# A fused attention and SwiGLU kernel: probabilities as the stationary operand, chunks of 256 queries, and an order from a list scheduler in the builder

## The chip, the cores and the metric

The kernel runs on one core of one Trainium2 chip. The metric is device time in microseconds (us), lower is better. Three runs of the kernel before stood at the outset: median 364.23 us, from 361.57 to 364.9.

Short names: PE is the matmul engine, PEld its weight load, DVE the vector engine, ACT the scalar engine, POOL the GpSimd engine, SP the engine whose queue stores the output. "AV" is the product of the attention probabilities with V; "FFN" is the gated network after the attention.

## The reference

Four batches, eight heads, 768 positions, head width 64. Attention has a block mask of 32x32 blocks (neighbours, first and last block row and column, three sampled blocks for each row). The result goes through an RMS norm and a gated network without bias. In short form:

```python
scores = scale * np.matmul(q, k.transpose(0, 1, 3, 2))     # 4 x 8 x 768 x 768
scores = np.where(mask, scores, -1000000000.0)
attn = np.exp(scores - np.max(scores, axis=-1, keepdims=True))
attn = attn / (np.sum(attn, axis=-1, keepdims=True) + 1e-09)
attn_out = np.matmul(attn, v)
x = attn_out.transpose(0, 2, 1, 3).reshape(B * S, H * D)   # 3072 x 512
rms = np.sqrt(np.mean(x * x, axis=-1, keepdims=True) + 1e-06)
xn = x / rms * rms_g
g = xn @ w_gate                                            # 512 x 1536
out = (g * (1.0 / (1.0 + np.exp(-g))) * (xn @ w_val)) @ w_out
```

## The kernel before

It works in eight units of 384 queries. For each pair of heads it computes the transposed scores (keys on the partitions, queries in the columns), takes the exponential on ACT, multiplies by a 0/1 mask on DVE, and then uses the result as the moving operand of AV:

```python
    def qk_mm(n, jt):
        # ... cut ...
        for e in range(2):                       # two heads: two 64-row halves of the array
            nc.tensor.matmul(
                out=s_[:, e, 0:TG],              # TG = 384 queries
                lhsT=x[64 * e:64 * e + 64, 1, jt, pr, :],
                rhs=x[64 * e:64 * e + 64, 0, ic * NT:(ic + 1) * NT, pr, :],
                start=True, stop=True)

    def av(n, shared):
        # ... cut ...
        for jt in range(NC):
            for e in range(2):
                nc.tensor.matmul(
                    out=o_[64 * e:64 * e + 64, :],
                    lhsT=vb[:, 2 * pr + e, jt * D:(jt + 1) * D],     # V is stationary, 64 columns
                    rhs=pt_[:, jt, e, :], start=(jt == 0), stop=(jt == NC - 1),
                    skip_group_check=True)
        nc.scalar.copy(out=osb[u][:, pr, :], in_=o_)
        # ... cut ...
```

The result has the head dimension on the partitions and the queries in the columns, as the FFN wants it. But the sum of a query's probabilities is then a sum over partitions. It takes matmuls of its own, which stream all probabilities through the array a second time:

```python
    def zsum(n):
        # ... cut ...
        for j2 in range(NC // 2):
            for e in range(2):
                for par in range(2):
                    c = 2 * e + par
                    nc.tensor.matmul(
                        out=zwt[u][32 * c:32 * c + 32, :], lhsT=Ez[:, pr, :],
                        rhs=pt_[:, 2 * j2 + par, e, :],
                        start=(pr == 0 and j2 == 0), stop=False, skip_group_check=True)
```

Five more functions (norm_a to norm_e) turn these sums and the squares into one factor per query and head, transpose the factors with matmuls (zt, ft), spread them over the partitions with matmuls (fb), and multiply. The FFN then runs with 384 moving columns for gate and value (gp, vp) and 512 for the output (yp). The order of work on PE is fixed by hand: steps with a list of costs, with the FFN of the unit before filling the gaps.

```python
        at(s1 + 1, 1.25, av, n, n >= 8)
        at(s1 + 1, 0.7, zsum, n)
```

The softmax here doesn't subtract the row's maximum and nothing guards it: scores larger than these inputs give would overflow.

## Time and profile before

| | before |
|---|---|
| time, median of the runs | 364.23 us |
| span of the profiled execution | 362.5 us |
| PE busy | 333.8 us (92%) |
| first FFN matmul (gp) starts | 54.94 us |
| one unit of 384 queries, steady | 40.0 us |

The profile's page gives, in this order: the span, the busy time of each engine, the PE's busy tenths in 40 slices with the clock granted to PE in the same slices, and the shares by engine of the chain that ended last.

```profile
span 362.5 us, 6294 instructions
...
PE 333.8 (92%) x2454; PEld 159.1 (44%) x2454; DVE 246.9 (68%) x531; ACT 222.6 (61%) x354; POOL 84.5 (23%) x112
...
PE   2787789899799999999999999999999999999995
...
PEclk9998988999999999999999999999999999999999
...
PE 75%; ACT 11%; DVE 7%; issue 4%; DMA 1%; POOL 1%; POOLq 0%; ACTq 0%; DVEq 0%
```

One warning for every clock figure of these views: time for which the trace has no clock record is counted as full clock. In this trace the record begins at 23.8 us, and the first two digits of the clock row say nothing.

PE is busy nearly everywhere after the first quarter, and the chain that ended last is 75% PE. The first quarter is worse: 2, 7, 8, 7, 7, 8, 9 tenths. The table of windows confirms it for two stretches of 40 us. Its columns are the stretch, its length, the busy time of PE, PEld, DVE, ACT and POOL (instructions in brackets), the granted clock, the DMA share and the GB/s.

```profile
180.00:220.00 40.00, 39.34 (x297) 18.87 (x293) 28.79 (x62) 27.61 (x45) 8.56 (x9) 1.00 0.56 90
220.00:260.00 40.00, 39.34 (x297) 18.87 (x293) 28.79 (x62) 27.61 (x45) 5.00 (x5) 1.00 0.06 21
```

39.34 of 40 us on PE, at full clock, against less than 29 on every other engine: in this state only less PE work, or the small rest, can gain time. The timeline shows what PE works on. Its columns are the start, the duration (both us), the engine, the line, the operation and its shapes. Durations of single matmuls contain a modelled end, so a cost is read from one start to the next.

```profile
200.61 1.17 PE L281 MATMUL o__2597<-pt,vb 128*64 128x384 bf16 x12
...
201.71 0.67 PE L297 MATMUL zw<-pt,Ez 128*32 128x384 bf16 x12
...
202.31 0.34 PE L248 MATMUL s__2626<-qkT 64*128 64x384 bf16 x2
...
202.48 0.33 PE L248 MATMUL s__2630<-qkT 64*128 64x384 bf16 x2
...
202.74 0.39 PE L419 MATMUL yp<-wo,hp 128*128 128x512 bf16 x1
```

AV takes 201.71 - 200.61 = 1.10 us per pair of heads and unit, the sums zw 202.31 - 201.71 = 0.60 us. The second score tile takes 0.26 us to the next full-array matmul where the first took 0.17 to the second: the other 0.09 us is a turn from 64-row score work to full-array work. The first FFN work, in the same view:

```profile
54.06 0.32 PE L368 MATMUL fb_726<-fs,SelB 128*128 128x384 bf16 x1 [0.20 <-DVE xn L373]
54.94 1.46 PE L388 MATMUL gp<-xn,wg 128*128 128x384 bf16 x4
```

Until 54.94 us there is no FFN work to fill PE's gaps.

### The profile page before, as it was taken

How to read it: one execution, taken by the hardware profiler on the slowest of the kernel's cores; microseconds unless marked ns; L12 is line 12 of the kernel's file. 1: busy time of each engine (PE TensorE's matmuls, PEld its weight loads, DVE VectorE, ACT ScalarE, POOL GpSimd, SP SyncE). 2: the span in 40 equal slices, each digit the busy share in tenths (PEclk: the TensorE clock that was granted, in tenths of full speed). 3: DMA queues.
4: the chain of work that ended last, by engine and by line, in shares of the span. 5: the costliest groups of instructions: out<-in, count | busy, mean ns of one | idle time of the engine just before them, and what ended most of it. 6: DMA issues, size and time to landing. Idle time of an engine off the chain costs nothing.

```text
span 362.5 us, 6294 instructions
## 1 busy us (share of the span) xinstructions
PE 333.8 (92%) x2454; PEld 159.1 (44%) x2454; DVE 246.9 (68%) x531; ACT 222.6 (61%) x354; POOL 84.5 (23%) x112
## 2 busy tenths in 40 slices
PE   2787789899799999999999999999999999999995
PEld 1233334344344444455444444454444444555552
DVE  3577786778666786687667785687767776666540
ACT  2465876777676667667666766766676675323321
POOL 8930620135331201143440311021011111100000
PEclk9998988999999999999999999999999999999999
DMA  5999999349661491067770390000000000000012
GB/s 64 171 213 198 157 189 159 72 29 59 44 40 36 104 161 55 32 43 74 73 61 15 62 225 33 32 0 32 29 29 1 31 29 3 30 31 29 33 56 88
DMA packets 69026, 25.58 MB, mean 71 GB/s; under 512 B 57220, under 2 KB 64900, under 8 KB 68996
## 3 DMA queue, kind: packets, MB, share of 16 engines
q0 software_dynamic: 46352, 14.16, 36.9%
q1 hardware_dynamic: 22644, 11.02, 13.0%
q8 instruction: 19, 0.31, 0.4%
q14 instruction: 11, 0.09, 0.1%
HBM read 28.31 MB, written 6.29 MB: 95 GB/s over the span
## 4 chain that ended last, share of the span: by engine, by line
PE 75%; ACT 11%; DVE 7%; issue 4%; DMA 1%; POOL 1%; POOLq 0%; ACTq 0%; DVEq 0%
PE yp L419 16%; PE gp L388 15%; PE vp L405 12%; ACT pt L256 6%; PE zw L297 5%; PE oa L281 3%; ACT th L392 3%; DVE uu L394 2%; DVE pt L262 1%; PE zt L317 1%; DMA kb<-in_k_dram 1%; PE fb L368 1%; DVE xn L373 1%; PE vw L405 1%; PE gw L388 1%
## 5 line engine op out<-in xcount | busy, mean ns | idle before, releaser
L262 DVE TENSOR_TENSOR pt<-pt,Mk 128x768 bf16<-128x768 bf16 x192 | 101.1, 571 | 0.4
L394 DVE SCALAR_TENSOR_TENSOR uu<-th,gp 128x384 bf16<-128x384 bf16 x90 | 49.8, 554 | 61.7 <-ACT th L392 61.4
L388 PE MATMUL gp<-xn,wg 128*128 128x384 bf16 x360 | 74.0, 328 | 3.1 <-DVE uu L394 2.9
L419 PE MATMUL yp<-wo,hp 128*128 128x512 bf16 x288 | 76.1, 380 | 0.0
L392 ACT ACTIVATE th<-gp 128x384 bf16<-128x384 f32 x90 | 44.4, 493 | 49.8 <-PE gp L388 46.8
L405 PE MATMUL vp<-xn,wv 128*128 128x384 bf16 x360 | 73.4, 326 | 0.7 <-DVE hp L408 0.6
L408 DVE TENSOR_TENSOR hp<-uu,vp 128x384 bf16<-128x384 bf16 x90 | 49.6, 551 | 10.2 <-PE vp L405 4.7
L388 PEld LDWEIGHTS <-wg 128*128 128x128 bf16 x384 | 35.5, 98 | 39.4 <-issue 14.5
L405 PEld LDWEIGHTS <-wv 128*128 128x128 bf16 x384 | 35.4, 98 | 29.9 <-issue 9.7
L419 PEld LDWEIGHTS <-hp 128*128 128x128 bf16 x288 | 26.1, 98 | 29.1 <-issue 7.7
L248 PEld LDWEIGHTS <-qkT 64*128 64x128 bf16 x384 | 13.9, 94 | 47.1 <-issue 45.5
L281 PEld LDWEIGHTS <-vb 128*64 128x64 bf16 x384 | 24.5, 115 | 16.8 <-issue 11.1
L425 ACT ACTIVATE yo<-yp 128x512 f32<-128x512 f32 x24 | 14.3, 597 | 13.6 <-PE yp L419 12.1
L297 PE MATMUL zw<-pt,Ez 128*32 128x384 bf16 x384 | 22.6, 344 | 0.0
L373 DVE SCALAR_TENSOR_TENSOR xn<-osb,gcol,fb 128x384 bf16<-128x384 f32 x28 | 15.9, 609 | 8.2 <-PE fb L368 8.2
L79 POOL DMA_DIRECT2D qb<-in_q_dram x18 | 16.4, 909 | 7.7 <-DMA wg<-in_moe_w_gate_dram 7.5
L79 POOL DMA_DIRECT2D qb<-in_k_dram x18 | 16.2, 901 | 7.1 <-DMA wv<-in_moe_w_val_dram 6.5
L332 POOL TENSOR_TENSOR rs<-ms,nhalf 128x3 f32<-128x3 f32 x8 | 7.1, 891 | 39.9 <-DVE ms L329 39.9
L297 PEld LDWEIGHTS <-Ez 128*32 128x32 bf16 x384 | 7.5, 97 | 12.8 <-issue 11.2
L281 PE MATMUL oa<-pt,vb 128*64 128x384 bf16 x96 | 12.6, 413 | 0.2 <-DVE Mk L199 0.2
L287 POOL TENSOR_TENSOR o_3107<-osb 128x384 bf16<-128x384 f32 x4 | 4.1, 1032 | 29.2 <-ACT osb L286 29.2
L287 POOL TENSOR_TENSOR o_2595<-osb 128x384 bf16<-128x384 f32 x4 | 4.1, 1030 | 28.3 <-ACT osb L286 28.3
(556 smaller groups left out, 415.6 us busy)
## 6 DMA issues: line engine op xcount, KB each, us to landing
out_dram<-yo SPq DMA_DIRECT2D x24, 256.0 KB, 2.0
vb<-in_v_dram POOLq DMA_DIRECT2D x4, 768.0 KB, 9.0
qb<-in_q_dram POOLq DMA_DIRECT2D x18, 128.0 KB, 4.5
qb<-in_k_dram POOLq DMA_DIRECT2D x18, 128.0 KB, 4.6
wg<-in_moe_w_gate_dram POOLq DMA_DIRECT2D x1, 1536.0 KB, 14.1
wv<-in_moe_w_val_dram POOLq DMA_DIRECT2D x1, 1536.0 KB, 20.7
wo<-in_moe_w_out_dram POOLq DMA_DIRECT2D x1, 1536.0 KB, 18.5
qb<-in_q_dram POOLq DMA_DIRECT2D x2, 192.0 KB, 3.6
```

The source lines that it names most:

```text
L79: nc.gpsimd.dma_start(out=flat[:, c * DM:(c + 1) * DM].rearrange("p (h d) -> p h d", h=H), in_=src[b, :, :, c * D:(c + 1) * D])
L256: nc.scalar.activation(out=ptiles[n][:, jt, :, :], in_=s_[:, :, 0:TG], func=AF.Exp, scale=SCALE)
L262: nc.vector.tensor_tensor(out=pv, in0=pv, in1=Mk[:, jt, ic * TG:(ic + 1) * TG].unsqueeze(1).to_broadcast([P, 2, TG]), op=ALU.mult)
L281: nc.tensor.matmul(out=o_[64 * e:64 * e + 64, :], lhsT=vb[:, 2 * pr + e, jt * D:(jt + 1) * D], rhs=pt_[:, jt, e, :], start=(jt == 0), stop ...
L297: nc.tensor.matmul(out=zwt[u][32 * c:32 * c + 32, :], lhsT=Ez[:, pr, :], rhs=pt_[:, 2 * j2 + par, e, :], start=(pr == 0 and j2 == 0), stop ...
L373: nc.vector.scalar_tensor_tensor(out=xns[u][:, pr, :], in0=osb[u][:, pr, :], scalar=gcol[:, pr:pr + 1], in1=fb[i], op0=ALU.mult, op1=ALU.mult)
L388: nc.tensor.matmul(out=gp, lhsT=wg[:, c, f * P:(f + 1) * P], rhs=xns[u][:, c, :], start=(c == 0), stop=(c == NP - 1))
L392: nc.scalar.activation(out=th, in_=gp, func=AF.Tanh, scale=0.5)
L394: nc.vector.scalar_tensor_tensor(out=uu, in0=th, scalar=1.0, in1=gp, op0=ALU.add, op1=ALU.mult)
L405: nc.tensor.matmul(out=vp, lhsT=wv[:, c, f * P:(f + 1) * P], rhs=xns[u][:, c, :], start=(c == 0), stop=(c == NP - 1))
L408: nc.vector.tensor_tensor(out=hps[u][:, f, :], in0=uu, in1=vp, op=ALU.mult)
L419: nc.tensor.matmul(out=yp, lhsT=hps[u][:, f, t * P:(t + 1) * P], rhs=wo[:, f, :], start=(f == 0), stop=(f == NF - 1))
```

## The change

Its intent is to have the sums for nothing. If a block of 128 queries of the probabilities is the stationary operand and V moves, the result has the queries on the partitions, and a column of ones appended to V gives the sum of probabilities as one more column. The division is then a multiplication by one value per partition and head. For the FFN the result must be transposed, which costs eight transposes for 256 queries. The core, with cuts:

```diff
+    va = [const.tile([P, H, NC, D + 2], BF16, name=f"va{i}") for i in range(2)]   # V and ones
 ...
-                nc.tensor.matmul(
-                    out=o_[64 * e:64 * e + 64, :],
-                    lhsT=vb[:, 2 * pr + e, jt * D:(jt + 1) * D],
-                    rhs=pt_[:, jt, e, :], ...)
+        for qt in range(2):
+            for e in range(2):
+                for jj in range(2):
+                    jt = 2 * j2 + jj
+                    nc.tensor.matmul(
+                        out=o_[:, qt, e, 0:D + 1],
+                        lhsT=pt[:, j2, e, jj * CQ + qt * P:jj * CQ + (qt + 1) * P],
+                        rhs=va[(ch // NIC) % 2][:, 2 * pr + e, jt, 0:D + 1], ...)
 ...
-    def zsum(n): ...
-    def norm_a(u): ...      # and norm_b to norm_e: zw, zt, ft, fb
+    def o_norm(ch, pr):     # DVE: rz = 1 / sums; x1 = o_ * rz
+    def square(ch, qt):     # ACT: sum of squares
+    def rstd(ch):           # POOL: (ms + eps) ** -0.5
+    def scale_x(ch, qt):    # DVE: x2 = x1 * rs, to bf16
+    def x_transposes(ch):   # PE: xT, eight transposes of 128x128
+    def x_copy(ch):         # DVE: xn = xT * g
 ...
-    TG = S // 2             # 384 queries, 8 units
+    CQ = 256                # 256 queries, 12 chunks
```

The second part is the order. In place of the steps set by hand, the builder holds every piece of work as a task with its engines, a price in microseconds, the tasks that it needs, and tokens for its buffers. A list scheduler plays the program with these prices and emits the instructions in the order that results. The engines keep that order, whatever the real durations are.

```diff
+    def dve1(n):
+        return n / 960.0 + 0.065
+    def dve2(n):
+        return n / 1920.0 + 0.065
+    def act(n):
+        return n / 1200.0 + 0.055
+    def pe(cols, n=1):
+        return n * (cols / 2400.0 + 0.0025)
 ...
+    SOLO = 144
+    runs = [TILES[i:i + 1] for i in range(SOLO)]          # score tiles issued one by one,
+    runs += [TILES[i:i + 2] for i in range(SOLO, len(TILES), 2)]   # the rest in pairs
 ...
+        plan.add(f"av{n}", {"PE": 8 * 0.0292}, lambda e, t=(ch, pr, j2): av(t), ...)
+        plan.add(f"rs{ch}", {"POOL": 0.25}, lambda e, ch=ch: rstd(ch), ...)
```

There are 144 score tiles, so SOLO = 144 means that none is planned as a pair. The start is new as well: the first chunk's loads come first, eight matmuls on zeros run before anything else, and V of batch 0 is loaded whole and copied by POOL next to the ones.

## The prediction

> **What bounds the kernel now.** The matmul engine. The page gives PE 333.8 of 362.5 us (92%); the table of windows gives 39.1 to 39.75 of every 40 us from 100 to 340 us at clock 1.00, DVE near 29, ACT near 27.6. One unit of 384 queries takes 40.0 us (ft copies start at 124.9, 164.8, 204.8, 244.8). The start is poor: the first gate matmul (gp) runs at 54.9 us, and PE idles 21 of the first 100 us.
>
> **Prices from the timeline (start to start).** A 384-column matmul 163 ns, 512 columns 216 ns, 128 columns behind its own 128x128 weight load 55 ns: columns/2.4 + 2.5. So, estimated, 256 columns 109 ns and 65 columns 29.6 ns. Turning from 64-row score pairs to full-array work, or back, leaves about 90 ns. Old AV takes about 1.1 us of PE per head pair, the zw sums 0.6.
>
> **Removed:** zw sums, 32 x 0.6 = 19 us; norm matmuls (zw<-o2, zt, ft, fb), about 2 us per unit, 15 us. **Added:** 96 transposes of xn (5.4 us), small DVE operations (reciprocal, two multiplies per head pair), squares on ACT. **Changed:** AV becomes 1152 matmuls of 65 columns, each with a 128-column weight load: 34 us against 35. This rests on the load hiding. The Trainium skill, "TensorE: Matmul & The Clock Gate" (Weight-path perf modes), says that 128-column non-FP32 weights load fast; the trace agrees: 128-column loads for the scores start 12 ns apart, old 64-column loads 25 to 28 ns. The same page (Back-to-back issue gap) has 81 ns per 128-column load-and-matmul; this trace has 55, which I use. Scores (31 us) and FFN (188 us) keep their columns; the order shows 116 visits to score mode against 96.
>
> **Sum.** PE work in the new order is 287 us, of which 274 from the first xn transpose (xT) on; steady chunks are 23.7 us per 256 queries, against 40.0 x 2/3 = 26.7 now. DVE (12 masks and 12 PSUM operations of 0.6 each, small ones: about 19 us per chunk) and ACT (16) stay under PE.
>
> **Start.** Chunk 0 needs only 12 exps, and its loads come first; V lands near 17 us, POOL copies it, xT follows near 28 us, the first gp near 30, instead of 55. One new wait: in POOL's order the rs of chunk 1 stands behind 18 loads of the next batch. Before, POOL waited 7.5 and 6.5 us for old loads to land before issuing more, so rs comes near 53 us, while PE wants xT of chunk 1 at 51: some 4 us of stall.
>
> **Total:** 28 + 274 + 4 (that stall) + 5 (2% idle of PE) + 3 (last yo and store) = 314 us. All of it is on the critical path, as PE is. About 25 us of the gain come from the start, the rest from PE work less new stalls.
>
> **Chances:** faster by over 2%: 0.96; within 2%: 0.02; slower: 0.02. Range 302 to 329.
>
> **What would show it.** AV matmuls 30 ns apart within a group; gp first at 28 to 33 us; chunk to chunk 24 to 25 us; PE over 96% busy from 60 us on; a POOL gap before rs of chunk 1, PE waiting at xT.
>
> **What would make it wrong.** AV at 53 ns (load not hidden): +27 us. The fixed order misjudging durations: with three banks for g, v, y and xT, and one for AV, late evacuation stalls PE in order (+10 to 20). Loads for batch 1 later than 55 us. Below 302 only if the rs wait vanishes and PE never idles.

## The result

| | before | changed |
|---|---|---|
| time, median of four runs | 364.56 us (361.57 to 364.92) | 326.16 us (325.57 to 327.46) |
| span of the profiled execution | 362.5 us | 323.9 us |
| PE busy, and its matmuls | 333.8 us, 2454 | 304.8 us, 3368 |
| first gp starts | 54.94 us | 37.46 us |
| from there to the end | 307.6 us | 286.4 us |
| steady, per 256 queries | 40.0 x 2/3 = 26.7 us | 24.2 to 24.3 us |

The ratio is 0.8961, with a 95% interval from 0.8915 to 0.9006. The result is correct. Of the 38.6 us of span that were gained, 54.94 - 37.46 = 17.5 lie before the first gate matmul and 307.6 - 286.4 = 21.2 after it. The first part is not idle time saved at the start: at its first gp the kernel before had done 80 of its 384 score matmuls and 60 of its 384 AV matmuls, the changed kernel 56 of 576 and 96 of 1152. PE had been busy for 43.7 us by then and idle for 11.3, against 28.3 and 9.2. Over the whole span PE's busy time fell by 29.0 us and its idle time, up to its last matmul, from 24.6 to 15.0 us.

The page of the changed kernel, the same lines as before:

```profile
span 323.9 us, 8037 instructions
...
PE 304.8 (94%) x3368; PEld 204.2 (63%) x3389; DVE 249.4 (77%) x533; ACT 214.3 (66%) x296; POOL 76.5 (24%) x107
...
PE   6875999997999999999999999999999999999995
...
PEclk9995699999999999999999999999999999999999
...
PE 82%; DVE 9%; ACT 3%; POOL 2%; issue 2%; DMA 1%; POOLq 0%; DVEq 0%; ACTq 0%
```

PE still holds the chain, now with 82%. The busy row is at 9 from the fifth slice on (except one 7), where before that took until the twelfth. The clock row has a new dent: 5 and 6 tenths in the fourth and fifth slices. The windows:

```profile
20.00:40.00 20.00, 14.66 (x177) 10.17 (x174) 14.36 (x37) 10.50 (x17) 7.23 (x9) 0.66 1.22 208
...
180.00:220.00 40.00, 39.79 (x435) 25.61 (x439) 32.36 (x72) 29.40 (x42) 1.85 (x4) 1.00 0.06 21
220.00:260.00 40.00, 39.89 (x467) 27.42 (x468) 33.24 (x69) 28.59 (x39) 0.93 (x2) 1.00 0.06 21
```

In steady state PE's idle part of 40 us went from 0.66 to 0.21 and 0.11 us, though DVE rose from 28.8 to about 33. At the start PE is busy 14.66 of 20 us, and the granted clock averages 0.66. A stretch of the steady timeline:

```profile
196.09 0.39 PE L448 MATMUL s__3368<-qkT 64*128 64x256 bf16 x4
...
196.41 0.67 PE L479 MATMUL o__3375<-va,pt 128*128 128x65 bf16 x16
...
196.92 1.03 PE L608 MATMUL gp<-xn,wg 128*128 128x256 bf16 x8
...
197.89 0.39 PE L448 MATMUL s__3403<-qkT 64*128 64x256 bf16 x4
```

Sixteen AV matmuls take 196.92 - 196.41 = 0.51 us, which is 32 ns each. Over all of them the pace is 32 ns in the median and 31.6 in the mean. Eight matmuls of 256 columns take 0.97 us to the next score tile. That is eight times 109 ns, and 0.10 us for the turn. The score tiles stand alone, each with a turn into score mode and one out of it. The steady prices over the whole trace, start to start:

| | predicted | measured |
|---|---|---|
| 65 columns behind a 128-column load | 29.6 ns | 31.6 ns (mean) |
| 256 columns | 109 ns | 109 ns |
| 512 columns | 216 ns | 216 ns |
| one transpose of xT | 55 ns | 56 ns |
| turn into score mode, and out of it | 90 ns | 96 and 93 ns |

And the start, where a note in brackets gives the idle time before the instruction and what ended it:

```profile
32.77 1.33 PE L525 MATMUL xT<-ident,x 128*128 128x128 bf16 x8 [3.62 <-DVE x L515]
...
35.92 0.61 PE L448 MATMUL s__547<-qkT 64*128 64x256 bf16 x4
...
37.46 1.08 PE L608 MATMUL gp<-xn,wg 128*128 128x256 bf16 x8
...
39.34 0.39 PE L448 MATMUL s__597<-qkT 64*128 64x256 bf16 x4
```

The first xT comes at 32.77 us, after 3.62 us of idle PE, behind the scaling of x on DVE. The eight transposes then last 1.33 us as recorded (a part of which is the second half of the scaling), and a group of four score matmuls 0.61 us; at 39.34 the same group takes 0.39. So the array was slow here in fact, not only in the record of the clock. The view of the first 20 us says 1.00, and yet the groups of four score matmuls took 0.61 us until 16 us, and 0.40 only from 17 us on. The Trainium skill, "TensorE: Matmul & The Clock Gate" (Seeing it yourself), warns that these clock events were seen to be unreliable on trn2; this trace does not agree. Its record begins at 17.08 us, with full clock, falls to a half at 23.91 and is full again from 37.56 on, and the matmuls change their pace at 17.0, 23.9 and 37.5. What misleads is the 1.00 for the time before the record begins.

After the first xT, all of PE's gaps over 0.1 us sum to 3.65 us in the remaining 287; 1.55 of them stand before the xT of chunk 2 (chunks are counted from 0). The stall that had been predicted at the rs of chunk 1 did not come. POOL's part of the timeline:

```profile
54.05 0.88 POOL L412 DMA_DIRECT2D va<-in_v_dram  x1 [0.47 <-DMA qb<-in_q_dram]
57.24 0.40 POOL L508 TENSOR_SCALAR rs<-ms 128x2 f32<-128x2 f32 x1 [2.30 <-ACT junk L502]
```

and ACT's:

```profile
56.95 0.20 ACT L502 ACTIVATION_READ_ACCUMULATOR junk<-x 128x1 f32 x1
```

POOL had issued its last load of batch 1 by 54.93 us, stood idle for 2.30 us, and started rs when ACT's squares were ready. The loads do make POOL wait, as the groups of the page show, but those waits fell before rs was due:

```profile
L208 POOL DMA_DIRECT2D qb<-in_q_dram x18 | 15.8, 922 | 6.4 <-DMA wo<-in_moe_w_out_dram 5.6
```

One more thing stands out at the start. While POOL copied V, two masks on DVE took 1.13 and 1.95 us instead of 0.68. POOL's timeline and DVE's, for the same stretch:

```profile
16.10 3.76 POOL L308 COPY va<-vraw 128x1536 bf16<-128x1536 bf16 x2 [0.69 <-DMA vraw<-in_v_dram]
```

```profile
17.41 3.59 DVE L466 TENSOR_TENSOR pt<-pt,Mk 128x1024 bf16<-128x1024 bf16 x3
```

Three masks in 3.59 us, where 2.1 would do.

### The profile page after: what moved, and what is told of

Read it like the earlier page. It is cut to its first block, busy times and chain, and to the rows that moved or that the text cites. A ratio compares the mean times of both kernels' runs of the same rounds, so it can differ in the third digit from the quotient of the medians.

```text
span 323.9 us, 8037 instructions
## 1 busy us (share of the span) xinstructions
PE 304.8 (94%) x3368; PEld 204.2 (63%) x3389; DVE 249.4 (77%) x533; ACT 214.3 (66%) x296; POOL 76.5 (24%) x107
## 4 chain that ended last, share of the span: by engine, by line
PE 82%; DVE 9%; ACT 3%; POOL 2%; issue 2%; DMA 1%; POOLq 0%; DVEq 0%; ACTq 0%
PE yp L642 20%; PE gp L608 18%; PE vp L608 18%; DVE pt L466 3%; PE xT L525 1%; PE tq L328 1%; ACT junk L502 1%; DMA kb<-in_k_dram 1%; DVE uu L622 1%; ACT pt L459 1%; DVE hp L632 1%; DVE x L494 1%; PE mp L375 1%; DVE x L515 1%; POOL rs L510 1%
## 5 line engine op out<-in xcount | busy, mean ns | idle before, releaser
L466 DVE TENSOR_TENSOR pt<-pt,Mk 128x1024 bf16<-128x1024 bf16 x144 | 98.5, 698 | 10.1 <-ACT pt L459 8.9
L608 PE MATMUL vp<-xn,wv 128*128 128x256 bf16 x576 | 74.8, 273 | 0.2 <-DVE hp L632 0.2
L608 PE MATMUL gp<-xn,wg 128*128 128x256 bf16 x576 | 74.7, 273 | 0.1
L618 ACT ACTIVATE th<-gp 128x512 bf16<-128x512 f32 x72 | 43.1, 599 | 34.4 <-PE gp L608 34.4
L608 PEld LDWEIGHTS <-wv 128*128 128x128 bf16 x576 | 53.5, 98 | 11.9 <-issue 4.9
L622 DVE SCALAR_TENSOR_TENSOR uu<-th,gp 128x512 bf16<-128x512 bf16 x72 | 49.1, 683 | 15.0 <-ACT th L618 14.6
L608 PEld LDWEIGHTS <-wg 128*128 128x128 bf16 x576 | 52.5, 98 | 9.2 <-issue 2.3
L479 PEld LDWEIGHTS <-pt 128*128 128x128 bf16 x1152 | 45.8, 99 | 18.4 <-issue 7.8
L632 DVE TENSOR_TENSOR hp<-uu,vp 128x512 bf16<-128x512 bf16 x72 | 49.2, 684 | 6.3 <-PE vp L608 2.6
L642 PEld LDWEIGHTS <-hp 128*128 128x128 bf16 x288 | 24.6, 97 | 26.2 <-issue 4.6
L515 DVE TENSOR_SCALAR x<-x,rs 128x512 bf16<-128x512 f32 x24 | 11.9, 536 | 15.6 <-POOL rs L510 15.6
L208 POOL DMA_DIRECT2D kb<-in_k_dram x18 | 16.3, 924 | 3.0 <-DMA qkT<-kb 3.0
## 6 DMA issues: line engine op xcount, KB each, us to landing
wo<-in_moe_w_out_dram POOLq DMA_DIRECT2D x1, 1536.0 KB, 29.6
```

The source lines that it names most:

```text
L208: nc.gpsimd.dma_start(out=flat[:, c * DM:(c + 1) * DM].rearrange("p (h d) -> p h d", h=H), in_=src[b, :, :, c * D:(c + 1) * D])
L466: nc.vector.tensor_tensor(out=pv, in0=pv, in1=m.unsqueeze(1).to_broadcast([P, 2, 2 * CQ]), op=ALU.mult)
L479: nc.tensor.matmul(out=o_[:, qt, e, 0:D + 1], lhsT=pt[:, j2, e, jj * CQ + qt * P:jj * CQ + (qt + 1) * P], rhs=va[(ch // NIC) % 2][:, 2 * p ...
L608: nc.tensor.matmul(out=pp[:, i * CQ:(i + 1) * CQ], lhsT=w[:, c, f * P:(f + 1) * P], rhs=xns[u][:, c, :], start=(c == 0), stop=(c == KC - 1))
L618: nc.scalar.activation(out=ths[u, fp], in_=gst[u, fp], func=AF.Tanh, scale=0.5)
L622: nc.vector.scalar_tensor_tensor(out=uus[u, fp], in0=ths.pop((u, fp)), scalar=1.0, in1=gst.pop((u, fp)), op0=ALU.add, op1=ALU.mult)
```

## The experiments

Theory A says that the time is the length of PE's own work from the moment that xT can start: matmul pace, turns of mode, and the little idle time that the planned order leaves. The AV weight loads are hidden, so what is taken from that work, or added to it, is seen in the time at full size. The rivals (theory B, in the form that each expectation gives it) hold that something else carries the gain or the shortfall: weight loads, the cold clock at the start, the lock between POOL and DVE, or the loads. Ten kernels were run. Each was timed beside the kernel before, and the ratio given is against it. The first four ran on one chip, the next four on a second and the last two on a third, so two runs are called different here only where the intervals of their ratios lie apart. "The changed kernel" stands at 326.16 us and 0.8961.

### Score tiles in pairs

```diff
-    SOLO = 144
+    SOLO = 0
```

> Score tiles two to a visit throughout: 72 visits to the 64-row score mode in place of 116. Theory A (PE is the bound, and each visit costs about 0.19 us of turning in and out): 44 x 0.19 = 8.3 us less, so about 318 us, chunk to chunk 23.4 us in place of 24.2. Rival B (pairs need both score buffers free at once, so PE now waits for ACT): time within 2 us of the changed kernel's 326, and PE gaps ended by ACT exps in front of score matmuls.

Measured: 320.55 us (319.59 to 321.96), ratio 0.8831 [0.8781, 0.8882], correct. There are 72 visits to score mode in place of 116. The timeline of this kernel shows a pair:

```profile
198.75 0.39 PE L448 MATMUL s__3464<-qkT 64*128 64x256 bf16 x4
...
198.98 0.38 PE L448 MATMUL s__3469<-qkT 64*128 64x256 bf16 x4
```

The second tile starts 0.23 us behind the first, where a tile alone took about 0.32 us to what followed. From chunk to chunk it is 23.3 to 23.4 us (24.2 to 24.3 in the changed kernel), as theory A has it. The gain was 5.6 us where 8.3 was expected. The first xT came at 35.0 instead of 32.8 us, but the first gp at 37.8 against 37.46, and the run of late pairs alone, below, has the early xT again and is no faster. The traces show the shortfall elsewhere: from the xT of chunk 5 on to that of chunk 11 pairs save 6.9 us (144.9 against 138.0), before that nothing (that xT comes at 143.97 against 143.07). Why the middle chunks do not gain is not shown.

### AV weights of 127 columns

This kernel is wrong (relative error 0.113): in five of six AV matmuls the stationary operand has 127 columns.

```diff
+                    m = P if jt == 0 else P - 1
-                        out=o_[:, qt, e, 0:D + 1],
-                        lhsT=pt[:, j2, e, jj * CQ + qt * P:jj * CQ + (qt + 1) * P],
+                        out=o_[0:m, qt, e, 0:D + 1],
+                        lhsT=pt[:, j2, e, jj * CQ + qt * P:jj * CQ + qt * P + m],
```

> Five of six AV matmuls load 127 columns of probabilities in place of 128; row 127 of each group of queries is wrong on purpose. Theory A (128-column weights load by a fast path, and only that hides the load behind 65 columns; otherwise one column takes one cycle at 2.4 GHz, as the 64-column loads of the kernel before did in 25 to 28 ns): pace of these matmuls 53 ns or more in place of 31.6, 960 x 22 ns = +21 us or more, about 347. [...] Rival B (any load hides behind the matmul before it): pace 30 to 32 ns, time unchanged at 326.

Measured: 352.9 us (351.38 to 355.61), ratio 0.9741 [0.9667, 0.9814]. The timeline of this kernel:

```profile
203.99 0.61 PE L480 MATMUL o__3190<-va,pt 128*127 128x65 bf16 x8
...
204.44 1.03 PE L643 MATMUL yp<-wo,hp 128*128 128x512 bf16 x4
```

Eight matmuls of 65 columns now take 0.45 us to the next work, and over the trace such matmuls stand 59 to 60 ns apart instead of 31.6. 960 matmuls times 28 ns is 27 us, and the time rose by 26.7. So theory A holds here in both halves: a PE cost of this kind is seen at its full size, and the change lives from the weight load of exactly 128 columns. This is what the Trainium skill, "TensorE: Matmul & The Clock Gate" (Weight-path perf modes), says of 128-column weights that are not FP32: they load fast. The same page's section LDWEIGHTS gives about P/1.2 ns for a load of P columns, an estimate of 106 ns at this width; a pace of 60 ns for load and matmul together rules that out as a cost per matmul here.

### Zero matmuls before the first xT

```diff
+    for dep, many in (('av0_0_2', 3), ('av0_1_2', 3), ('av0_2_2', 3), ('av0_3_2', 12)):
+        for w in range(many):
+            plan.add(f"w_{dep}_{w}", {"PE": 0.22}, lambda e: nc.tensor.matmul(
+                out=fbank("warm"), lhsT=idle[:, 0:P], rhs=idle, start=True, stop=True),
+                deps=[">" + dep], acq=["f"], rel=["f"], mode="f", prio=30)
```

> 21 matmuls of zeros fill PE's waits between 19 and 33 us. Theory A (the waits let the granted clock fall to half from 24 to 37 us, and the cold PE lengthens the last AVs of chunk 0, xT and what stands before the first gp): clock 1.00 in that stretch, xT of chunk 0 about 1 us earlier (31.8), first gp about 2.5 us earlier (35), time 323 to 324. Rival B (the start is bound by the chain of DVE, ACT and POOL, not by PE's clock): clock up, but first gp within 0.7 us of 37.5 and time unchanged.

Measured: 324.69 us (322.69 to 325.82), ratio 0.8936 [0.8892, 0.8981], correct. The window of this kernel that answers to the first one above:

```profile
20.00:40.00 20.00, 18.53 (x231) 11.87 (x228) 14.83 (x37) 12.05 (x19) 7.23 (x9) 1.00 1.22 208
```

The view says 1.00 (0.66 before), but this trace's record begins at 23.51 us, and the matmuls were slow up to 23.4 us and fast after. In the changed kernel it was the other way round: fast from 17.0 to 23.9 us, then slow. Two lines of this kernel, an AV group that is still slow and the first xT:

```profile
22.30 1.43 PE L484 MATMUL o__361<-va,pt 128*128 128x65 bf16 x24
...
32.74 0.40 PE L530 MATMUL xT<-ident,x 128*128 128x128 bf16 x4 [0.47 <-DVE x L520]
```

The first xT starts at 32.7 us in both; the first gp starts at 36.33 in place of 37.46. The median fell by 1.5 us, but the intervals of the ratios overlap. A fast array shortens the way from xT to gp by 1.1 us (3.60 in place of 4.69). Whether PE's speed moves xT as well, this run cannot tell, since the array was slow before 23.4 us; the run of late pairs and zero matmuls below can. Behind the last AV of the chunk stands a chain without PE: the division on DVE, the squares on ACT, rs on POOL, the scaling on DVE, from 29.2 to 32.7 us. The added tasks also shifted the order of DVE and ACT a little, so the run does not change the clock alone.

### V loaded straight into place

```diff
-    vraw = raw.tile([P, H, NC * D], BF16, name="vraw")
-    for lo in (0, 4):
-        nc.gpsimd.dma_start(out=vraw[:, lo:lo + 4, :], in_=vv[0, :, lo:lo + 4, :])
+    for c in range(NC):
+        nc.gpsimd.dma_start(out=va[0][:, :, c, 0:D], in_=vv4[0, :, :, c, :])
 ...
-    V_AT = (15.0, 17.6)     # and the two POOL copies are gone
+    V_AT = (18.5, 18.5)
```

> V of batch 0 is loaded by six DMAs straight into the tile with the ones columns; POOL copies nothing. Theory A (while POOL copies V, a mask multiplication on DVE waits for the copy to end: two masks took 1.13 and 1.95 us instead of 0.68, and the chunk-0 chain runs over DVE): masks back to 0.68 us each, xT of chunk 0 about 1.5 us earlier, time about 324.5. Rival B (those waits are off the chain, or the smaller DMA elements bring V later and eat the gain): masks 0.68 us but time within 0.7 us of 326.

Measured: 329.24 us (328.63 to 330.28), ratio 0.9069 [0.9029, 0.9108], correct: a miss, 3 us slower than the changed kernel. On DVE and PE:

```profile
17.92 0.68 DVE L463 TENSOR_TENSOR pt<-pt,Mk 128x1024 bf16<-128x1024 bf16 x1
```

```profile
21.74 1.50 PE L476 MATMUL o__330<-va,pt 128*128 128x65 bf16 x24
```

The masks do take 0.68 us now. But V was complete only at 20.25 us (the copies were done at 17.99 and 19.87), the first AV started at 21.74 (18.77), the gate weights landed at 24.4 (22.1), and the first xT came at 35.9. The array was slow from 8.9 to 43.1 us by the record of this execution, also where that of the changed kernel was fast (17.1 to 23.9). The run changes too much at once to say which of these cost the 3 us. Taking away the cause of the lock by a slower path for V does not pay; that is all that it shows.

### The kernel before with a third of its sums

This one changes the kernel before, and is wrong (relative error 0.030):

```diff
-        for j2 in range(NC // 2):
+        for j2 in range(1):
 ...
-        at(s1 + 1, 0.7, zsum, n)
+        at(s1 + 1, 0.25, zsum, n)
```

> The kernel before, with only 4 of the 12 zw row-sum matmuls per head pair (the sums, so the result, are wrong on purpose). Theory A (the kernel before is bound by PE, so the work that the change removed was on the critical path): 2 groups of four concurrent matmuls less, 2 x 0.163 us x 32 head pairs = 10.4 us, so about 353 us. Rival B (in steady state the kernel before waits for DVE and ACT as much, and the gain of the change comes from its new order and start): within 3 us of 364.

Measured: 360.83 us (358.44 to 361.29), ratio 0.9925 [0.9849, 1.0002], where 353 was expected: some 3 us, and not clear of noise. From the third to the seventh copy of ft, four units, it took 155.1 us against 159.9 in the kernel before. That is 1.2 us for each unit. By matmuls, two times 163 ns are gone for each head pair, 1.30 us for the four of a unit: in steady state the removed work is seen nearly whole. A new wait took a part of it, and PE's busy share fell a little. The timeline shows the second score tile of a step behind its buffer:

```profile
213.47 0.34 PE L248 MATMUL s__2609<-qkT 64*128 64x384 bf16 x2
...
214.10 0.34 PE L248 MATMUL s__2613<-qkT 64*128 64x384 bf16 x2 [0.29 <-DVE xn L373]
```

Such waits, counted from start to start, rose from 0.11 to 1.06 us for each unit, while others fell: PE's idle time in all rose from 0.73 to 0.88 us for each unit. The rest was lost at both ends. The first gp came at 57.4 us (54.9); the record, which begins at 23.6 us, has the array slow from 27.0 to 30.4 and from 33.8 to 61.2 us here, and in the kernel before only three times for 3.4 us. From the seventh copy of ft to the end it took 78.9 us (77.7). So theory A holds in steady state and misses the ends, which took back 2.5 and 1.2 us; why the start was later was not tested. All eight units could give 8 x 1.30 = 10.4 us for two thirds of the sums, or 15.6 for all of them. The sums are thus a part of the 38 us that the change gained, and not the larger one.

### Half prices in the builder

The same instructions as in the changed kernel, in another order: the scheduler believes DVE and ACT to be twice as fast.

```diff
-        return n / 960.0 + 0.065
+        return 0.5 * (n / 960.0 + 0.065)
-        return n / 1920.0 + 0.065
+        return 0.5 * (n / 1920.0 + 0.065)
-        return n / 1200.0 + 0.055
+        return 0.5 * (n / 1200.0 + 0.055)
```

> The changed kernel, but the list scheduler in the builder believes that all DVE and ACT work takes half its time; the instructions are the same, only their order differs. Theory A (the order, chosen with prices near the measured ones, is what lets three shared banks feed PE without waits): PE stalls in order behind late evacuations, 10 us or more slower, 336 or more, PE windows under 97%. Rival B (buffers are deep enough that any sensible order keeps PE fed): within 3 us of 326.

Measured: 362.81 us (361.86 to 364.02), ratio 1.0002 [0.9939, 1.0064], correct. The whole gain is gone. A window of this kernel:

```profile
200.00:240.00 40.00, 35.70 (x400) 23.27 (x397) 30.11 (x62) 25.78 (x35) 0.93 (x2) 1.00 0.04 14
```

and a line of its timeline:

```profile
206.53 0.42 PE L479 MATMUL o__3148<-va,pt 128*128 128x65 bf16 x8 [0.72 <-DVE pt L466]
```

PE idles about 4 of 40 us, and 39.6 in all against 15.0 in the changed kernel, at waits such as this one: AV stands in PE's order where the plan thinks that the mask is done, the mask is not done, and PE can do nothing else. From chunk to chunk it is 27.5 us. Prices at half cost 362.81 - 326.16 = 37 us, as much as the whole change gained. The step is far larger than theory A had expected.

### Pairs after the first chunks, and the zero matmuls

Pairs only from the 24th score tile on keep the single tiles at the start, where the first run's xT came later. The zero matmuls are the same as above.

```diff
-    SOLO = 144
+    SOLO = 24
+    # and the 21 zero matmuls of the third run
```

> Single score tiles for the first 24, pairs after that (73 visits to score mode), and the zero matmuls that keep the clock up at the start. If the two gains add: 43 x 0.19 = 8.2 us from visits and 1.5 us as in the run with zero matmuls alone: 316.5 us, and the chunk-0 xT back at 32.7 us from the 35.0 of the run with pairs from the first tile. If the pairs cost the start again: 319 to 320.

Measured: 319.14 us (318.4 to 319.33), ratio 0.8793 [0.8754, 0.8833], correct, with 73 visits to score mode. Steady chunks take 23.3 to 23.4 us, the first xT comes at 31.9 us and the first gp at 35.5. The same two places as in the first run with zero matmuls:

```profile
21.97 0.92 PE L484 MATMUL o__361<-va,pt 128*128 128x65 bf16 x24 [0.69 <-DVE x L499]
...
31.89 0.40 PE L530 MATMUL xT<-ident,x 128*128 128x128 bf16 x4 [0.47 <-DVE x L520]
```

Up to the first xT the order on PE, DVE, ACT and POOL is the same in these two traces. In this one the array is fast from 18.8 us on, in the other from 23.4 on, and xT comes 0.85 us earlier. So PE's speed does move xT, as far as one execution of each can show it. From the end of the last AV to xT it is 3.6 us in both.

The time is short of the 316.5 that a plain sum of the effects gave. Here is where some of it stays:

```profile
78.93 0.61 PE L530 MATMUL xT<-ident,x 128*128 128x128 bf16 x8 [1.91 <-DVE uu L627]
```

PE waits 1.91 us ahead of the third xT, and 0.82 ahead of the fourth. The release named here is a DVE operation of the FFN, uu, which is the last reader of a gp bank, and xT takes one of the same three banks. Right behind this wait the record has the array at half clock from 79.8 to 83.2 us, and the matmuls are slow there: eight gate matmuls take 1.85 us from start to start. Between the xT of chunk 1 and that of chunk 5 PE works 82.6 us, where the run of late pairs alone, without such a stretch, has 81.1.

### POOL fills V by a memset

Wrong (relative error 0.724). POOL stays busy (memsets of 1.4 us in place of copies of 1.8 to 1.9) but reads almost nothing:

```diff
-            out=va[0][:, 4 * h2:4 * h2 + 4, :, 0:D], in_=vraw[...]
+            out=va[0][:, 4 * h2:4 * h2 + 4, :, 0:1], in_=vraw[...][:, :, :, 0:1]),
+            nc.gpsimd.memset(va[0][:, 4 * h2:4 * h2 + 4, :, 1:D], 0.05)),
```

> POOL fills batch 0's V tile with a constant (one small copy keeps the wait for V's load; the result is wrong on purpose); all else and the order stay. Theory A (what stops DVE is a POOL instruction that reads SBUF while DVE reads two SBUF operands): POOL as busy as before at 16 to 20 us, yet all masks take 0.68 us; xT of chunk 0 up to 1.5 us earlier, time 324.5 to 326. Rival B (any POOL work on the shared port, writes too, stops it): masks of 1 to 2 us again, time 326.

Measured: 326.52 us (325.13 to 327.47), ratio 0.8996 [0.8951, 0.9041]. On POOL and on DVE, in the same stretch:

```profile
16.01 1.38 POOL L311 MEMSET va<- 128x1512 bf16 x1
...
18.03 1.39 POOL L311 MEMSET va<- 128x1512 bf16 x1
```

```profile
17.33 0.68 DVE L467 TENSOR_TENSOR pt<-pt,Mk 128x1024 bf16<-128x1024 bf16 x1
18.44 0.69 DVE L467 TENSOR_TENSOR pt<-pt,Mk 128x1024 bf16<-128x1024 bf16 x1 [0.43 <-ACT pt L460]
```

All masks take 0.68 or 0.69 us, also the one that overlaps the second memset. So it is not a busy POOL that holds up the mask, but a POOL operation that reads SBUF. This agrees with the Trainium skill, "SBUF — State Buffer" (SBUF: two separate sides), which says that a DVE operation with two SBUF inputs and a GpSimd operation that reads SBUF exclude each other from a shared pair of ports. The masks have two SBUF inputs. But the first xT came at 32.9 us and the time did not move. The run of late pairs alone, below, is the fair partner: up to the first xT it has the same order on PE, DVE and ACT and nearly the same states of the array (slow until 22.1 us, here 22.4, then fast until 29), two masks of 1.13 and 1.65 us, and its first xT comes at 32.86 against 32.93 here. The lock is real and costs nothing measurable here.

### Measured prices in the builder

The kernel of late pairs and zero matmuls, with four prices set to what the traces show:

```diff
-        plan.add(f"av{n}", {"PE": 8 * 0.0292}, ...
+        plan.add(f"av{n}", {"PE": 8 * 0.0316}, ...
-        plan.add(f"rs{ch}", {"POOL": 0.25}, ...
+        plan.add(f"rs{ch}", {"POOL": 1.0}, ...
-            plan.add(f"sc{ch}_{qt}", {"DVE": dve2(512)}, ...
+            plan.add(f"sc{ch}_{qt}", {"DVE": 0.42}, ...
-        plan.add(f"xc{ch}", {"DVE": 4 * dve2(256)}, ...
+        plan.add(f"xc{ch}", {"DVE": 1.1}, ...
```

> As the run with late pairs and zero matmuls (319.1 us), but four prices in the builder are set to what the trace shows: rs on POOL 1.0 us (it believed 0.25), one scaling of x 0.42 (0.33), four copies of xT 1.1 (0.79), eight AV matmuls 0.253 (0.234). Theory A (PE's waits of 1.9 us at 77 us and 0.8 us at 103 us come from places where the plan believed xT or AV ready too early): those waits shrink to under 0.5 us, time 316 to 317.5. Rival B (they come from the first chunks' loads or from chance of a greedy order): time 318 to 321, waits elsewhere.

Measured: 312.68 us (310.97 to 313.03, five runs), ratio 0.8594 [0.8563, 0.8626], correct. It beats both kernels. The third xT and the windows of this kernel:

```profile
79.13 0.61 PE L530 MATMUL xT<-ident,x 128*128 128x128 bf16 x8
```

```profile
40.00:80.00 40.00, 38.45 (x488) 27.76 (x486) 35.25 (x77) 33.41 (x47) 14.52 (x19) 1.00 1.73 130
...
160.00:200.00 40.00, 40.00 (x484) 29.12 (x482) 33.81 (x74) 29.34 (x40) 1.59 (x3) 1.00 0.08 28
```

The wait ahead of this xT is gone. PE is busy 38.45 us between 40 and 80 (36.66 in the run of late pairs and zero matmuls) and without a gap from 120 to 280 us. Chunks take 22.9 to 23.0 us. Against the trace with the old prices, 2.5 us come from waits between the xT of chunk 1 and that of chunk 5, some 1.6 from less PE work there, as the slow stretch behind the third xT is missing now, 2.2 from the six chunks after that, and 1.0 from the end; 0.5 are lost up to the first xT and 0.8 more up to the second. The four prices were not tried one by one, so which of them does it is open. The shorter steady chunk at the same instructions is an effect of the order too.

### Late pairs alone

```diff
-    SOLO = 144
+    SOLO = 24
```

> Late pairs alone, without the zero matmuls. If the two are additive: 326.2 - 8.2 = 318 to 320.5, xT of chunk 0 at 32.8 us as in the changed kernel, first gp at 37.5; and 1 to 1.5 us above a version with zero matmuls. If the zero matmuls are worth nothing with pairs: 319 as with them.

Measured: 320.25 us (319.69 to 320.63), ratio 0.8816 [0.8784, 0.8847], correct. The first xT comes at 32.9 us and the first gp at 37.5, as in the changed kernel, and steady chunks take 23.3 to 23.4 us. So late pairs are worth 5.9 us by themselves. That is no more than pairs from the first tile on (320.55 us; the intervals overlap), though the first xT is 2.1 us earlier: the single tiles at the start did not pay. The zero matmuls on top of them are worth 320.25 - 319.14 = 1.1 us by the medians, but these intervals overlap too.

## Why the prediction was right, and where it was off

The direction and the range were right: 314 us predicted, 302 to 329 given, 326.16 measured, so of a gain of 50 us three quarters came. There was luck in it: most terms were too low, by 17.5 us together, and the forecast stall that did not come, with less other idle time, took back 5.4. Without that the sum would have been 331.5, outside the range. Term by term, in the terms that the prediction used (the first column is its own):

| term | predicted | measured |
|---|---|---|
| until the first xT | 28 | 32.8 |
| PE work from there on | 274 | 283.4 |
| stall at rs of chunk 1 | 4 | 0 |
| other idle time of PE | 5 | 3.65 |
| after the last matmul | 3 | 4.0 |
| outside the profiled span | 0 | 2.3 |
| sum | 314 | 326.2 |

The measured PE work is a difference: PE's last work ends at 319.85 us, less 32.77, less 3.65 of idle time. The last line is the 326.16 of the median less the 323.87 of the span; 0.6 of it is that the profiled execution, at 325.57, was faster than the median.

- Right: PE bounds both kernels. PE is busy 39.8 and more of 40 us in steady state, and doubling the cost of an AV matmul (the run with 127 columns) raised the time by just what PE lost. In the kernel before, 1.30 us less PE work for each unit took 1.2 us off it.
- Right: the weight loads of AV are hidden. 30 ns were predicted, and 32 (median) and 31.6 (mean) measured. The 53 ns named as what would make the prediction wrong came in the run with 127 columns, as 59 to 60 ns, with its 27 us.
- Right: chunk to chunk 24 to 25 us, measured 24.2 to 24.3. PE over 96% busy from 60 us on: 255.8 of the 260 us up to 320, though only 17.9 of the first 20.
- Right in size, not in every reason: "about 25 us of the gain come from the start" was 17.5, and 21.2 of the other 25 came after the first gp. And most of the 17.5 is PE work that is not done yet at the first gp (28.3 us against 43.7), not time in which PE had idled.
- Wrong: the step "PE wants xT of chunk 1 at 51: some 4 us of stall". There was none. POOL was through with its loads at 54.93, and rs waited 2.30 us for ACT's squares. PE did not wait at xT of chunk 1, which ran at 59.41. The loads were out nearly when predicted (rs was expected at 53), but chunk 1 itself was later, so that rs fell due after them.
- Mis-sized: "xT follows near 28 us, the first gp near 30". Measured 32.77 and 37.46. The prediction followed loads and copies, and not the chain from AV through DVE, ACT, POOL and DVE to xT, which waits its turn in each engine's order. From xT to gp it allowed 2 us where 4.7 passed, as the planned order puts transposes and scores of the next work there, at a slow array. In the run with zero matmuls it was 3.60 us. What fixes xT itself at 32.8 is open in part. From the last AV to xT it is 3.6 us in each trace, on DVE, ACT, POOL and DVE. Masks without the lock did not move it (32.93 against 32.86 in like states of the array); an array that was fast from 18.8 us on brought it to 31.9.
- Mis-sized: PE work from xT on, 283.4 against 274. About 2.1 us are AV at 31.6 instead of 29.6 ns (1056 matmuls after the first chunk). About 1.7 are the slow array between xT and gp (4.32 us of work, against 2.59 for the same matmuls in the run with zero matmuls). About 1.4, by estimate, is the first step within each score tile (119 to 120 ns against 109, in 132 tiles), and about 1 the turns at 93 and 96 ns against 90. Some 3 us are not assigned.
- Not foreseen: how much hangs on the prices. "The fixed order misjudging durations" was named as a risk of 10 to 20 us. The runs say 37 us for prices at half, and 6.5 us (319.14 to 312.68) for four prices put right. In the changed kernel the price of a mask is 0.60 us and the trace's mean 0.698: an error of a seventh still served, an error of more than a half did not.

Where the gain comes from can be stated as far as the runs carry it. Of the 38.6 us of span, 29.0 are PE's busy time and 9.5 its idle time; the idle part of a steady stretch shrank from 0.66 to 0.1 or 0.2 us in 40. The new products make the PE work smaller; the order makes it count. Neither is enough as tried here: leaving out two thirds of the sums in the old order gave some 3 us, not clear of noise, and the new products in a badly priced order gave nothing. Two runs that would split the gain were not made: the old products in an order from the scheduler, and the new ones in an order by hand. So how much belongs to each part is not shown.

## What to carry to other kernels

A list scheduler in the builder is only as good as its prices: take them from a trace of the kernel itself, above all for small operations, and take them again after each change, since the engines keep the planned order even where it is wrong. When the probabilities (or any operand) are to be stationary against few moving columns, give them exactly 128 columns, because one column less nearly doubled the cost of such a matmul here. Turns between half-array and full-array matmuls are paid each time, so put score tiles together; keeping them single at the start brought the first result 2.1 us earlier and the end no earlier. Before two traces are compared, look at where their clock records begin and where the array was slow: in the first 40 us this differed here even between kernels with the same order on PE (fast from 17.0, 22.1 and 22.4 us on).

## What the Trainium skill lacked or had wrong

- "TensorE: Matmul & The Clock Gate" (Back-to-back issue gap) says that in a stream of loads and matmuls the spacing is about 81 ns at 128 columns and 131 ns at 512. Here it was 56 ns and 216 ns. The same page's earlier figures for warm matmuls without a gap, 55.6 and 215.7 ns, fit; those of the stream do not.
- The same page (LDWEIGHTS, and Weight-path perf modes) does not say what a load of bf16 weights costs beside few moving columns. At 65 moving columns, load and matmul together took 31.6 ns with 128 stationary columns and 59 to 60 ns with 127; the formula for a load, P/1.2 ns for P columns or, by estimate, 106 ns here, was not seen as a pace.
- "TensorEngine Tiling (Array Packing)" (Key Properties) says that switching the mode requires a drain, and gives no figure. Here a turn from full-array work to 64-row score pairs cost 96 ns, and the turn back 93 ns.
- "TensorE: Matmul & The Clock Gate" (Seeing it yourself) calls the clock events unreliable on trn2. Here they held: in the changed kernel they change at 17.08, 23.91 and 37.56 us, and the matmuls change their pace at 17.0, 23.9 and 37.5. The page does not say that the events can begin late (at 17.08 us here, and at 40.92 in the run with half prices), so that a view that takes missing events for full clock says 1.00 over slow matmuls.
